# Where a kernel makes its last weight parts: eight in place of six behind the first batch's units

## The chip, the cores and the metric

The kernel runs on one core of a Trainium2 chip. The metric is the device time of one execution in microseconds (us). The engines are named as in the profile: PE is TensorE (PEld its weight loads), DVE is VectorE, ACT is ScalarE, POOL is GpSimd, SP is SyncE, which here only issues DMAs. Each engine works through its own list of instructions in the order written down at build time, and waits where an instruction's inputs or buffers aren't ready.

## What is computed

The input x has 8 batches of 3008 tokens with 256 channels. A real Fourier transform runs along the tokens, a complex 256 x 256 product with a bias and a soft threshold acts on the spectrum, and the inverse transform gives the tokens back. A feed-forward layer follows, with the square of a ReLU between its two products.

```python
X = np.fft.rfft(x, axis=1)
Yr = Xr @ w_r - Xi @ w_i + b_r
Yi = Xr @ w_i + Xi @ w_r + b_i
Yr = np.sign(Yr) * np.maximum(np.abs(Yr) - 0.01, 0.0)
Yi = np.sign(Yi) * np.maximum(np.abs(Yi) - 0.01, 0.0)
y = np.fft.irfft(Yr + 1j * Yi, n=3008, axis=1)
h = y.reshape(24064, 256) @ w_in          # 256 x 2048
out = np.maximum(h, 0.0) ** 2 @ w_out     # 2048 x 256
```

The weights w_in and w_out come as 64-bit floats.

## The kernel before

**The transforms.** 3008 is 64 x 47, so each transform is two stages of small matrix products with a pass through device memory between them. Batch 0 comes first and alone: seven `Fwd32` loads (`ring`) make its first stage, and 24 units (`Unit32`) do the rest, each with a load (`ka`), a forward product (`fwd`, L401), copies (`bins`), the mix with the weights (L415), the threshold on DVE (`shrink`, tiles `kv` and `kc`), and the way back (`back`, L426) with a store of two halves (`kuh`, `kul`) into the array `s3`. Later batches do the same as `Fwd` or `Fwd2` tasks and as pairs of units (`Pair`), spread as jobs with due times in half steps between the feed-forward work of the batch before. For batch 1, `Fwd2` runs thirteen times (L352): the first five directly behind the units, from x loaded early (`x6`), the other eight in the first tile, from the two buffers of `xt`.

**The feed-forward layer.** Each batch is cut into six tiles of some 500 tokens. `Back` loads a tile's data from s3 (`du`), makes the last stage of the inverse transform on PE (L461, L464, L465), and ACT and DVE write it to `yr` (through `dy`). `Tokens` forms the sums (`ms`) and the two halves (`yt`) that the products need; for the first tile DVE does this, for the others POOL. A tile has eight steps and each step two half steps, `first` and `second`: seven products in the manner of Strassen-Winograd, each of three matmuls, out of `win` into the banks `psh`. DVE reads these (`mp`, `mu`, `mv`, `mc`), ACT makes ReLU, square and a rounded copy (`mg`), POOL the rest of `mg`. `out` of step n, two steps later, multiplies with `wout` into `pso`. The steps' own instructions are chained in order on each engine by `then`.

**The weights.** w_in and w_out are cut into 16 parts of 128 x 512, in the order of the list `parts`: two of w_in, two of w_out, and so on. A part (`Double`) is loaded as 64-bit values (512 KB, tile `dst`, tag `big`, four buffers), and `convert(n, after)` makes 32-bit floats of it. `bits` is one ACT and four DVE instructions (L148 to L155), `join` two on DVE (L159 and L163), after which the loaded tile is no longer needed. A part of w_out is then split into a rounded half and a rest (`split`, one instruction on ACT and one on DVE). For w_in this is done for two parts at a time (`win_sums`): four sums (`ds`) and three splits, seven instructions on DVE and three on ACT. `after` names a unit or step: `bits` is then placed behind that step's last DVE and ACT instruction (`cut` and `done`).

**Which part is made when.** Parts 0 and 1 are made before the units. `EARLY` and `LATE` set the rest: with `LATE = 6`, parts 2 to 9 are made behind every second unit (`paced`, turns 3 to 17 of the loop at L670), parts 10 to 12 behind the last unit, and parts 13, 14 and 15 behind half steps 1, 3 and 5 of the first tile (`LATER`). Parts 10 to 13 are loaded in turns 20 to 23 of the units' loop, each placed behind the load of a unit or of the last one; parts 14 and 15 are loaded behind the first tile's loads of `du`. All loads in question are on SP's queue, and those made through `load_next` (L106) are kept in one order: each is placed behind the one before it in `chain`. The loads of `xt`, and the `du` loads of later tiles, come behind the last weight loads in that chain.

**Memory and order.** A tag has a fixed number of buffers (`FRONT`, `MAIN`), and a tile takes a buffer when the last reader of the tile before is done. The weights' scratch lies in a pool `conv`; when the last part is placed the pool is closed (L748), and its memory goes to the tiles of the pairs and of `Fwd` named in `SIDE`. A planner turns the program into one list for each engine: of the instructions that are ready by its own estimate of time, it takes the one that stands first in the program, and obeys `issue_after`.

Of the kernel before, what the change touches and what calls it, by code (L numbers as in the profile page):

```python
# [58 lines left out]
def fnet_moe(ctx: ExitStack, tc, x, w_r, w_i, b_r, b_i, w_in, w_out, bm, cm, dx, a32, c32, out):  # L59
# [21 lines left out]
    def memory(stack, name, **kwargs):  # L81
        return stack.enter_context(tc.tile_pool(name=name, bufs=2, reuse_waits="tile", **kwargs))
# [89 lines left out]
    def moe_part(q):  # L172
        if q < 8:
            f, c = divmod(q, 2)
            return Double(
                None, None, w_in[c * 128:(c + 1) * 128, f * 1024:(f + 1) * 1024],
                lambda t: t.rearrange("p f t -> p (f t)"),
            )
        f = (q - 8) * 2
        return Double(  # L180
            wout[0][:, f:f + 2], wout[1][:, f:f + 2],
            w_out[f * 128:(f + 2) * 128, :].rearrange("(f p) d -> p f d", p=128),
            lambda t: t.rearrange("p (f d) t -> p f (d t)", f=2),
        )


    def win_sums(n, parts):
        (a11, a21), (a12, a22) = (
            [w[:, :, f] for f in range(2)]
            for w in (p.w.rearrange("p (n f d) -> p n f d", n=2, f=2) for p in parts)  # L190
        )
        st = T("ds", [128, 2, 4, 128], F32)
        s1, s2, s3, s4 = (st[:, :, j] for j in range(4))
        dve.tensor_add(out=s1, in0=a21, in1=a22)
        sub(dve, s2, s1, a11)
        sub(dve, s3, a11, a21)
        sub(dve, s4, a12, s2)
        hi, lo = (w[:, 2 * n:2 * n + 2] for w in win)
        halves(hi[:, :, A11], lo[:, :, A11], a11, dve)
        halves(hi[:, :, A12:A22 + 1], lo[:, :, A12:A22 + 1], parts[1].w.rearrange("p (n f d) -> p n f d", n=2, f=2), dve)  # L200
        halves(hi[:, :, S1:], lo[:, :, S1:], st, dve)
# [386 lines left out]
    def pair_tasks(pairs, start, step, end=7.1):  # L588
        jobs = []
        for j, u in enumerate(pairs):  # L590
            at = start + j * step
            if j:
                jobs += [(at - 3.7, u.load)]
            jobs += [
                (at, u.fwd), (at + 1.0, u.sums), (at + 3.7, u.load_back),
                (at + 2.1, lambda u=u: u.mix(1)), (at + 3.0, lambda u=u: u.mix(0)), (at + 4.0, u.shrink),
                (at + end, lambda u=u: u.back(0)), (at + end + 0.9, lambda u=u: u.back(1)),
            ]
        return jobs

    def fwd_tasks(b, start, step):
        jobs = []
        for q in range(J):
            f, at = Fwd(b, q), start + q * step
            jobs += [(at - 2.5, f.load), (at - 0.8, f.add), (at + 0.3, f.run)]
        return jobs

    def back_tasks(t, start):
        b, c0, h = tiles[t]
        new = range(-(-c0 // W2), -(-(c0 + 2 * h) // W2))  # L610
        jobs = []
        for j, q in enumerate(new):
            k, at = Back(b, q), start + 2.2 * j
            jobs += [(at, k.load), (at + 1.6, k.mm)]
            if len(k.spans) > 1:
                jobs += [(start + 14.6, k.put)]
        k = Tokens(t)
        for j in range(2):
            jobs += [(start + 7.1 + j, lambda j=j: k.sums(j))]
        for j in range(4):  # L620
            jobs += [(start + 9.1 + 1.2 * j, lambda j=j: k.split(j))]
        return jobs
# [8 lines left out]
    parts = [moe_part(q) for q in (0, 1, 8, 9, 2, 3, 10, 11, 4, 5, 12, 13, 6, 7, 14, 15)]  # L631
# [9 lines left out]
        b32 = load_mix_weights()  # L641


    EARLY, LATE = 2, 6
    LATER = {1: 13, 3: 14, 5: 15}

    def convert(n, after=None):
        p = parts[n]
        p.bits(after)
        p.join()  # L650
        if n % 4 > 1:
            p.split()
        elif n % 4:
            win_sums(n // 4, parts[n - 1:n + 1])
# [6 lines left out]
    for n in range(EARLY):  # L661
        convert(n)
    paced = [(n, 2 * (n - EARLY)) for n in range(EARLY, len(parts) - LATE)]
    loads = [(k - 1, parts[n]) for n, k in paced] + [(20 + j, p) for j, p in enumerate(parts[-LATE:-2])]

    PRE = 5
    nam = T("nam", [M1, M1], F32)
# [2 lines left out]
    for r in range(-5, len(units) + 3):  # L670
# [10 lines left out]
        while loads and loads[0][0] <= r:  # L681
            p = loads.pop(0)[1]
# [16 lines left out]
    steps = [Step(t, n) for t in range(len(tiles)) for n in range(NF // 2)]  # L699
    slots = len(HALF) * NF  # L700
    first = sorted(back_tasks(0, 0), key=lambda j: j[0])
    for name in ("load", "mm", None):
        for _, job in first:
            if (job.__name__ if job.__name__ in ("load", "mm") else None) == name:
                job()
        for p in parts[-2:] if name == "load" else ():
            with tc.issue_after(chain[nc.sync].ins):
                p.load()
            chain[nc.sync] = p.get
    for n in range(len(parts) - LATE, min(LATER.values())):  # L710
        convert(n, units[-1])
    nam = T("nam", [M1, M1], F32)
    act.mul(nam, am32[:, 1], -1.0)
# [3 lines left out]
    for m in range(2 * len(steps) + 4):  # L717
        b, r = divmod(m, slots)
        if r == 0 and b < B:
            jobs = [(t - slots, job) for t, job in jobs]  # L720
            if b + 1 < B:
                first, step, end = 1.0, 6.1, 7.1
                if b == 0:
                    first, step, end = 11.2, 5.3, 9.1
                    for q in range(PRE, J):
                        if q > PRE + 1:
                            jobs += [(0.9 * (q - PRE - 2), second[q].load)]
                        jobs += [(0.5 + 0.9 * (q - PRE), second[q].run)]
                    jobs += [(first - 0.6, pairs[1][0].load)]
                jobs += pair_tasks(pairs[b + 1], first, step, end)  # L730
            if b + 2 < B:
                first, step = (2.6, 7.0) if b else (14.6, 6.0)
                jobs += fwd_tasks(b + 2, first, step) + [(95.0, pairs[b + 2][0].load)]
            for j in range(len(HALF)):
                t = b * len(HALF) + j + 1
                if t < len(tiles):
                    jobs += back_tasks(t, NF * j + 0.5)
            jobs.sort(key=lambda j: j[0])
        n, k = divmod(m, 2)
        if k and 0 <= n - 2 < len(steps):  # L740
            steps[n - 2].out(1)
        if n < len(steps):
            (steps[n].second if k else steps[n].first)()
        if not k and 0 <= n - 2 < len(steps):
            steps[n - 2].out(0)
        if m in LATER:
            convert(LATER[m], steps[n])
        if m == max(LATER):  # L748
            conv.close()
            pools.update(dict.fromkeys(CONV), **dict.fromkeys(SIDE, memory(ctx, "side")))  # L750
        while jobs and jobs[0][0] < r + 1:
            jobs.pop(0)[1]()
# [86 lines left out]
```

## Time and profile before

| | us |
|---|---|
| median of 3 runs | 2615.43 |
| lowest and highest | 2613.71, 2618.53 |
| the profiled execution | 2614.82 |
| its span in the profile | 2613.1 |

The profiled execution is the one from which all rows come. A row of the timeline gives start, duration, engine (PEq, SPq and so on are the queues that issue), line, operation, what is written from what, the shapes, how many instructions the row holds, and in brackets how long the engine had been idle before it and what released it. A line can be that of a helper: L97, L98 and L101 are the copies and the subtraction that every part of the kernel calls, and L484 is `then`. A row of the view by stages gives busy time in a stretch. Each matmul of 32-bit floats outside the steps shows as two matmuls in a row.

### The profile page before, as it was taken

The page shows a single profiled execution, that of the slowest core. Times are in us where ns is not written, and L with a number is a line of the kernel's source. Part 1 is how long each engine was busy: PE and PEld are TensorE (multiplying, and loading weights), DVE is VectorE, ACT ScalarE, POOL GpSimd, SP SyncE. Part 2 cuts the span into 40 slices and gives each one's busy share as a digit, 9 for nine tenths or more (in the row PEclk, how much of TensorE's full clock was granted, in tenths as well). Part 3 has the DMA queues.
Part 4 walks back from the last instruction along what each step waited for, and adds up shares of the span by engine and source line. Part 5 has one row for each costly group of instructions (what it writes and reads, how often), then busy time and mean ns, then how long its engine had stood idle before and what let it go on. Part 6 is the DMA issues. An engine that isn't in the chain of part 4 may idle for free.

```text
span 2613.1 us, 47540 instructions
## 1 busy us (share of the span) xinstructions
PE 2564.3 (98%) x16908; PEld 2347.0 (90%) x16908; DVE 1782.3 (68%) x3797; ACT 1672.7 (64%) x2434; POOL 1657.0 (63%) x1628
## 2 busy tenths in 40 slices
PE   6799999999999999999999999999999999999999
PEld 4689989999999999999999999999999999999998
DVE  6877766667767767577676776667676677765554
ACT  3556656666666666666666666666666666666665
POOL 2246666766766667667666676666667666666564
PEclk8999999999999999999999999999999999999999
DMA  8733332333332332233332333323332223221100
GB/s 267 236 110 110 102 113 82 95 106 107 95 91 75 116 104 86 84 95 113 104 92 82 97 110 100 99 76 101 103 108 80 71 79 101 71 65 41 33 17 17
DMA packets 191455, 250.51 MB, mean 96 GB/s; under 512 B 21755, under 2 KB 135923, under 8 KB 191219
## 3 DMA queue, kind: packets, MB, share of 16 engines
q1 hardware_dynamic: 178240, 223.89, 28.1%
q0 software_dynamic: 12304, 22.35, 3.6%
q8 instruction: 136, 2.23, 0.4%
q10 hardware_dynamic: 675, 1.23, 0.2%
q14 instruction: 100, 0.82, 0.1%
HBM read 146.85 MB, written 100.53 MB: 95 GB/s over the span
## 4 chain that ended last, share of the span: by engine, by line
PE 84%; POOL 1%; DMA 1%; issue 0%; DVE 0%; ACT 0%; POOLq 0%; SPq 0%; ACTq 0%; DVEq 0%
PE pso L484 36%; PE psh L484 32%; PE psf L301 6%; PE psf L280 2%; PE psf L236 2%; PE psf L333 2%; PE psf L464 1%; PE psf L465 1%; PE psf L461 1%; DMA du<-s 1%; POOL mg L101 0%; POOL yt L101 0%; POOL ms L101 0%; POOL ms L500 0%; ACT mc L484 0%
## 5 line engine op out<-in xcount | busy, mean ns | idle before, releaser
L101 POOL TENSOR_TENSOR mg<-mc,mg 128x500 fp32r<-128x500 f32 (+1 forms) x768 | 975.0, 1290 | 594.3 <-ACT mg L97 549.7
L484 PE MATMUL pso<-mg,wout 128*128 128x500 f32 (+1 forms) x4608 | 1176.2, 392 | 1.8 <-ACT mg L97 1.3
L484 PE MATMUL psh<-yt,win 128*128 128x250 f32 (+1 forms) x8064 | 1072.9, 281 | 1.5 <-DVE mc L484 1.2
L484 ACT ACTIVATE mc<-mc 128x1000 f32<-128x1000 f32 (+1 forms) x768 | 802.6, 1045 | 406.6 <-DVE mc L484 397.3
L484 PEld LDWEIGHTS psh<-yt,win 128*128 128x128 f32 x8064 | 1022.2, 189 | 34.3 <-PE psh L484 1.9
L484 PEld LDWEIGHTS pso<-mg,wout 128*128 128x128 f32 x4608 | 818.7, 189 | 130.0 <-POOL mg L101 1.9
L484 DVE TENSOR_TENSOR mc<-psh,mv 128x500 f32<-128x500 f32 (+3 forms) x768 | 419.1, 547 | 428.1 <-PE psh L484 395.4
L97 ACT CAST mg<-mc 128x1000 fp32r<-128x1000 f32 (+1 forms) x384 | 396.9, 1034 | 18.4 <-ACT mc L484 0.4
L484 DVE TENSOR_TENSOR mv<-psh,mu 128x500 f32<-128x500 f32 (+1 forms) x384 | 260.6, 679 | 53.5 <-PE psh L484 21.8
L301 PE MATMUL psf<-wx,kxh 128*128 128x256 f32 x1008 | 206.7, 281 | 2.4 <-ACT kxh L97 1.7
L98 DVE COPY mp<-psh 128x250 f32<-128x250 f32 (+1 forms) x384 | 159.7, 416 | 39.2 <-PE psh L484 16.2
L301 PEld LDWEIGHTS psf<-wx,kxh 128*128 128x128 f32 x1008 | 166.3, 189 | 6.7 <-ACT kxh L97 1.9
L101 POOL TENSOR_TENSOR ksl<-kv,ksh 128x512 fp32r<-128x512 f32 x84 | 108.8, 1295 | 94.6 <-ACT ksh L97 94.5
L484 DVE TENSOR_TENSOR mu<-psh,mp 128x250 f32<-128x250 f32 (+1 forms) x384 | 160.5, 418 | 11.5
L215 POOL TENSOR_TENSOR xs<-xt 120x256 f32<-120x256 f32 x156 | 115.4, 760 | 72.5 <-DMA xt<-x_in 67.6
L484 DVE TENSOR_TENSOR mc<-psh,mp 128x250 f32<-128x250 f32 (+1 forms) x384 | 156.8, 408 | 4.3 <-PE psh L484 2.8
L322 DVE TENSOR_TENSOR kv<-psf,ke 64x256 f32<-64x256 f32 x336 | 141.8, 422 | 22.9 <-PE psf L301 14.2
L301 PE MATMUL psf<-wx,kxl 128*128 128x256 f32 x504 | 141.1, 280 | 1.0 <-DVE kxl L101 1.0
L97 ACT COPY dy<-psf 128x188 f32<-128x188 f32 x256 | 76.9, 313 | 82.7 <-PE psf L465 82.2
L313 DVE TENSOR_TENSOR ke<-psf,bias 128x512 f32<-128x512 f32 x84 | 58.0, 691 | 102.0 <-PE psf L301 101.9
L97 ACT CAST ksh<-kv 128x512 fp32r<-128x512 f32 x84 | 52.0, 619 | 114.3 <-DVE kv L101 113.4
L97 ACT CAST kuh<-psf 128x256 fp32r<-128x256 f32 x192 | 68.4, 372 | 88.2 <-PE psf L333 71.4
(102 smaller groups left out, 2565.4 us busy)
## 6 DMA issues: line engine op xcount, KB each, us to landing
du<-s SPq DMA_DIRECT2D x128, 256.0 KB, 2.9
s<-kuh SPq DMA_DIRECT2D x192, 128.0 KB, 1.8
s<-kul SPq DMA_DIRECT2D x192, 128.0 KB, 1.8
kcm<-cm_in POOLq DMA_DIRECT2D x84, 256.0 KB, 3.3
ka<-s SPq DMA_DIRECT2D x84, 256.0 KB, 3.4
s<-xe SPq DMA_DIRECT2D x87, 240.0 KB, 2.4
xt<-x_in SPq DMA_DIRECT2D x86, 240.0 KB, 3.3
du<-s SPq DMA_DIRECT2D x256, 64.0 KB, 2.8
```

What stands on the lines that cost most here:

```text
L97: return act.copy(out=out, in_=in_)
L98: return eng.tensor_copy(out=out, in_=in_)
L101: return eng.tensor_tensor(out=out, in0=a, in1=b, op=ALU.subtract)
L215: return eng.tensor_tensor(out=out[:, :n], in0=self.xt[:, :n, 0], in1=self.xt[:, :n, 1], op=(ALU.add, ALU.subtract)[t])
L236: nc.tensor.matmul(ps[:M1, t], am32[:, t], self.u[:, t], start=True, stop=True)
L280: nc.tensor.matmul(pv[:, :, c, g, :], self.a[:, g, c * 128:(c + 1) * 128], bg, start=True, stop=True)
L301: self.last = nc.tensor.matmul(ps, l, wx[j][:, k, c, :], start=n == 0, stop=n == 5)
L313: dve.tensor_add(out=self.e, in0=self.pe, in1=bias)
L322: dve.tensor_add(out=v[64 * r:64 * r + 64, g], in0=ps[gs], in1=self.e[gs, r])
L333: nc.tensor.matmul(ps[:, :D], self.cm[:, g, j * 128:(j + 1) * 128], r[:, g], start=n == 0, stop=n == 2)
L461: mm = nc.tensor.matmul(pv[:, :, 0], self.u[:, 0, cs], dx_sb[:, 0], start=True, stop=False)
L484: last_of[eng] = op(*args, **kwargs)
```

## The change

Parts 8 and 9, a pair of w_in, are no longer made between the units. `LATE` becomes 8, and `LATER` holds lists of parts. Parts 8 to 10 are made behind the last unit, part 11 behind half step 1 of the first tile, the pair 12 and 13 behind half step 3, part 14 behind half step 5 and part 15 behind half step 7. Parts 8 to 11 are loaded in turns 18 to 21 of the units' loop, and the last four parts behind the first tile's `du` loads. The pool `conv` is closed behind half step 7.

```diff
-    EARLY, LATE = 2, 6
-    LATER = {1: 13, 3: 14, 5: 15}
+    EARLY, LATE = 2, 8
+    LATER = {1: (11,), 3: (12, 13), 5: (14,), 7: (15,)}
...
-    loads = [(k - 1, parts[n]) for n, k in paced] + [(20 + j, p) for j, p in enumerate(parts[-LATE:-2])]
+    loads = [(k - 1, parts[n]) for n, k in paced] + [(18 + j, p) for j, p in enumerate(parts[-LATE:-LATE + 4])]
...
-        for p in parts[-2:] if name == "load" else ():
+        for p in parts[4 - LATE:] if name == "load" else ():
             with tc.issue_after(chain[nc.sync].ins):
                 p.load()
             chain[nc.sync] = p.get
-    for n in range(len(parts) - LATE, min(LATER.values())):
+    for n in range(len(parts) - LATE, min(LATER.values())[0]):
         convert(n, units[-1])
...
-        if m in LATER:
-            convert(LATER[m], steps[n])
+        for p in LATER.get(m, ()):
+            convert(p, steps[n])
         if m == max(LATER):
             conv.close()
```

## The prediction

> **What bounds the kernel now.** First the page's first part, for which engine sets the time.
>
> ```profile
> span 2613.1 us, 47540 instructions
> PE 2564.3 (98%) x16908; PEld 2347.0 (90%) x16908; DVE 1782.3 (68%) x3797; ACT 1672.7 (64%) x2434; POOL 1657.0 (63%) x1628
> ```
>
> TensorE (PE) is busy 2564.3 of 2613.1 us. The change adds and removes no matmul, so only the 48.8 us in which PE is idle, or runs at a reduced clock, can move. The view of busy time by stages tells where they are (columns: stretch, its length, then PE, PEld, DVE, ACT, POOL busy, granted clock, DMA share, GB/s).
>
> ```profile
> 60.00:82.00 22.00, 18.05 (x91) 15.73 (x92) 21.98 (x48) 11.91 (x34) 6.41 (x6) 1.00 0.91 283
> 82.00:110.50 28.50, 25.91 (x131) 22.34 (x130) 23.39 (x54) 13.78 (x41) 10.76 (x10) 1.00 0.71 227
> 110.50:119.40 8.90, 8.90 (x44) 7.56 (x43) 8.62 (x19) 5.66 (x11) 0.00 (x0) 1.00 0.70 217
> 119.40:130.60 11.20, 3.83 (x21) 3.09 (x19) 8.35 (x22) 4.92 (x13) 0.28 (x1) 0.74 0.75 227
> 130.60:136.10 5.50, 5.47 (x16) 4.32 (x17) 0.00 (x1) 0.59 (x1) 0.00 (x0) 0.60 0.11 26
> 136.10:187.50 51.40, 50.85 (x321) 45.77 (x320) 42.18 (x83) 33.79 (x48) 28.66 (x27) 1.00 0.45 131
> 355.00:366.00 11.00, 6.50 (x37) 5.52 (x36) 5.21 (x11) 6.11 (x11) 10.98 (x13) 0.89 0.58 162
> 366.00:2613.10 2247.10, 2239.70 (x14985) 2061.68 (x14984) 1512.62 (x3235) 1466.62 (x2065) 1475.99 (x1446) 1.00 0.29 86
> ```
>
> Up to 110.5 the units of batch 0 run; VectorE (DVE) is full from 60 to 82, but over 82 to 110.5 PE is short of only 2.6 us. From 110.5 to 130.6 lies the passage to the first tile. From 136.1 on PE is all but full: 0.55 us idle in the first tile's 51.4 us, 7.4 us in the last 2247. So the change can win at most what PE loses between 82 and 136, and it can lose in the first tile.
>
> **What leaves the units.** Parts 8 and 9 go from between the units to behind them. In the trace they run on DVE from 82.05 to 99.1, between the units' own work (tile kv); the second row below is that work alone. The three rows are the DVE rows of the view by stages: all, then the instructions on kv, then all in the passage.
>
> ```profile
> 82.05:99.10 17.05, 16.57 (x38) 1.00 0.77 237
> ...
> 82.05:99.10 17.05, 7.66 (x18) 1.00 0.77 237
> ...
> 110.45:121.35 10.90, 10.52 (x22) 1.00 0.71 213
> ```
>
> Of the 38 instructions, 18 are on kv and one is the last of part 7; the other 19 (six for each part, seven for the sums of the pair) take 16.57 - 7.66 - 0.7 = 8.2 us. DVE gives up 8.2 us here. PE does not gain as much, since it is already near its own pace:
>
> ```profile
> 86.75 0.67 PE L426 MATMUL psf<-kv,kk 128*128 128x256 f32 x2 [0.43 <-DVE kv L101]
> ...
> 92.67 0.67 PE L426 MATMUL psf<-kv,kk 128*128 128x256 f32 x2 [0.33 <-issue]
> ...
> 97.95 0.60 PE L426 MATMUL psf<-kv,kk 128*128 128x256 f32 x2
> ...
> 100.56 0.60 PE L426 MATMUL psf<-kv,kk 128*128 128x256 f32 x2
> ...
> 104.08 0.70 PE L426 MATMUL psf<-kv,kk 128*128 128x256 f32 x2 [0.75 <-ACT ku L97]
> ...
> 110.06 0.67 PE L426 MATMUL psf<-kv,kk 128*128 128x256 f32 x2 [0.96 <-DVE kv L101]
> 110.56 1.46 PE L352 MATMUL psf<-x,am 120*120 120x256 f32 x6
> 111.86 0.59 PE L352 MATMUL psf<-x,nam 120*120 120x256 f32 x2
> 112.29 1.46 PE L352 MATMUL psf<-x,am 120*120 120x256 f32 x6
> ```
>
> From 97.95 to 100.56 a unit costs 2.6 us with PE never waiting. The last gap (0.96) is the latency of the last unit's shrink and stays. The others shown, with some smaller ones, make 2.6 - 0.96 = 1.6 us. The 0.75 us at 104 waits for ScalarE, itself behind stores; loads of four parts still go out together behind the last unit's load, so that gap may stay. I take **-1.2 us** for this stage (between 0 and -2.6). Two 512 KB loads also leave this stage; I give them nothing of their own, since the gaps above already hold what they could win.
>
> **The passage.** Between the last unit and the first tile DVE did parts 10, 11 and 12 (the 22 instructions of the last row above, two of them kul: 20 in 10.1 us, 0.5 us each) and then two instructions of part 13. It now gets parts 8 and 9 with the seven sums, and 10: 26 instructions against 22, +2.0 us. It is not laid on the path whole. Behind the L352 runs, the path goes through the first tile's inverse transform:
>
> ```profile
> 122.61 0.36 PE L461 MATMUL psf<-dx_sb,du 128*128 128x188 f32 x1 [2.60 <-DVE yr L471]
> ...
> 124.39 0.33 PE L461 MATMUL psf<-dx_sb,du 128*128 128x188 f32 x1 [0.83 <-DMA du<-s]
> ```
>
> At 122.61 PE waited for DVE, which had been on weights until then; at 124.39 it waited 0.83 us for a transfer all the same. So 0.8 us more on DVE would be hidden there, and DVE itself waits again afterwards. In this stage DVE is busy 8.35 of 11.2 us, so 2.85 us are free, and 2.0 are added, low in priority against the tile's own work. I take **+0.8 us**: half an instruction of delay at a few places. Bounds: -1.7 (if the weights no longer stand ahead of yr at 122) and +2.0 (all on the path).
>
> **The first tile.** Parts 11 to 15 replace 13 to 15 here. The whole DVE, and then its step work fed from psh, in the stretch where 13 to 15 are made:
>
> ```profile
> 143.40:169.00 25.60, 24.99 (x45) 1.00 0.40 112
> ...
> 143.40:169.00 25.60, 8.02 (x18) 1.00 0.40 112
> ```
>
> 45 - 18 - 2 (yr, 0.5 us) = 25 weight instructions in 16.5 us: 0.66 us each, against 0.5 in the passage. Added are seven for part 11, six for 12 and the two of 13 that had slipped into the passage: 15, so 7.5 us (at 0.5) to 9.9 us (at 0.66). DVE has 51.4 - 42.2 = 9.2 us free from 136.1 to 187.5, and all 5.5 us from 130.6 to 136.1. This last hole exists because PE did two L352 runs of batch 1 (16 matmuls) before it went on with step 0; they waited for x, loaded at 125.00:
>
> ```profile
> 123.88 1.03 SPq L139 DMA_DIRECT2D dst<-w_out_in  x2
> 125.00 9.72 SPq L108 DMA_DIRECT2D xt<-x_in  x3
> ...
> 143.57 0.33 SPq L108 DMA_DIRECT2D xt<-x_in  x1
> ...
> 160.83 1.48 SPq L108 DMA_DIRECT2D du<-s  x3
> ...
> 176.31 0.42 DVE L98 COPY mp<-psh 128x252 f32<-128x252 f32 x1
> ...
> 169.63 1.11 POOL L108 DMA_DIRECT2D kcm<-cm_in  x2
> ...
> 177.86 0.39 SPq L108 DMA_DIRECT2D ka<-s  x1
> ```
>
> That order cannot stay. Four loads of weights now stand where two stood, and there are four buffers for them (tag big). Parts 8 to 11 fill these, so the load of part 15 has to wait until part 11 is joined, which is put behind step 0. The loads of x are chained behind it on SP, so the L352 runs must come after step 0, and steps 0 and 1 start some 5 us sooner. DVE so has 9.2 + 5.5 = 14.7 us for the 7.5 to 9.9 us added: it fits. PE's total work is the same, and what was two L352 runs at a clock of 0.60 (5.5 us for what takes 3.5 at 110.56) becomes step work at that clock, an even trade. Parts 12 and 13 together keep DVE from steps 2 and 3 for a time, while fewer L352 runs are at hand to fill PE; for that I take **+2 us** (between -2, if the earlier steps pay, and the slower cases below). All weights are in time: 12 and 13 are wanted by step 6, whose step work on DVE comes at 176.31 us, and 14 and 15 by outputs later still. The memory of the weights goes over to the pairs of batch 1 (names in SIDE) two half steps later: kcm at 169.63 on POOL's queue may be held until part 15 is done, ka at 177.86 on SP's by little; the pairs' first matmul comes after both, and I cost this at nothing as long as part 15 is done by 178, else at what it is late.
>
> **Sum.** -1.2 + 0.8 + 2.0 = +1.6 us. The profiled execution took 2614.8 us (1.7 around its span), so 2616.4; it lies 0.6 below the median of the three runs, so against that median **2617.0 us**. 0.2% is 5.2 us, about what a measurement can tell from no change.
>
> **A rule that speaks against the change.** In the first tile GpSimd (POOL) runs beside the weights, which the units' stage has less of. Mean times of one instruction in the first tile and then in the passage, where POOL did nothing:
>
> ```profile
> L151 DVE TENSOR_SCALAR da<-da 128x512 f32<-128x512 f32 x3 | 3.1, 1023 | 0.3 <-ACT da L148 0.3
> ...
> L151 DVE TENSOR_SCALAR da<-da 128x512 f32<-128x512 f32 x3 | 1.3, 425 | 0.3
> ```
>
> The instruction takes 2.4 times as long in the first tile, so a part moved there costs more than it did. The Trainium skill, page "SBUF — State Buffer", section "Who interferes with whom", says that VectorE's two-port modes and its instructions with two SBUF inputs share a port pair with GpSimd, and that the one that starts second blocks fully until the first ends; these two rows agree. By that rule alone, with every added instruction meeting POOL, rival C is what comes out.
>
> **Rivals.**
> A, *the units were DVE-bound after all*, and the passage loses its wait: then -2.6 and -1.7 and a gain of 2 in the first tile, 2615.4 - 6.3 = **2609**. For it: DVE full at 60 to 82. Against: PE's own 2.6 us a unit.
> B, *SP's queue*, on the slower side: the load of part 15 holds back x and, in the same chain, the tile-1 loads of du. A join took 8.4 us from the end of its step in the trace:
>
> ```profile
> 139.48 0.41 DVE L484 TENSOR_TENSOR mc<-psh,mp 128x252 f32<-128x252 f32 x1
> ...
> 147.63 0.68 DVE L159 SCALAR_TENSOR_TENSOR dw<-dst,da 128x512 f32<-128x512 uint32 x1
> ...
> 179.70 1.28 POOL L101 TENSOR_TENSOR yt<-ms,yt 128x504 fp32r<-128x504 f32 x1 [0.28 <-ACT yt L97]
> ...
> 185.55 1.81 PE L484 MATMUL psh<-yt,win 128*128 128x252 f32 x14
> ```
>
> With step 0 done near 135, x is loaded near 143.5 in place of 125.0: 18.5 us late. Tile 1's yt was ready at 181.0, and PE wants it at 186.6 (nine of the 14 matmuls at 185.55 still belong to tile 0): 5.6 us of slack. If nothing is caught up, PE stands 18.5 - 5.6 = 12.9 us; two buffers of x allow two runs in about 7 us, by which six runs before the last du load need 21 and put it at 164, 3 us late and hidden. It decides when the delay of that load passes 5.6 us. I price it at half, 6.5 us: 2615.4 - 0.4 + 6.5 = **2621.5**.
> C, *DVE runs out in the first tile*: if all 15 added instructions are slowed as L151 is, they take 15 x 0.5 x 2.4 = 18.0 us where 14.7 are free, and PE waits the other 3.3 us on top of the forecast: **2620.3**. For it: the 24.99 of 25.60 us above. Against: the mean of 0.66 us that holds for the 25 weight instructions there.
>
> **How the numbers follow.** Forecast 0.57 (2611 to 2620.5), A 0.14, B 0.16, C 0.13. The idle 4.5 us at 355 to 366 hang on the order that the planner writes down and may go or double: that widens both ends. Range 2609 to 2625: A's and B's times with the 12.9 us end of B cut short. Faster by over 0.2% (below 2610.2): A, 0.14. Slower by over 0.2% (above 2620.7): B and about half of C with a little of the forecast's own tail, 0.25. Within: 0.61.
>
> **What would show it.** Units: the last L426 at 108.5 to 109.5, not 110.06. Passage: yr near 121 to 122. First tile: no L352 ahead of step 0's end, DVE at work from 131 to 136, the load of part 15 followed by x near 143; PE idle of 2 to 3 us between 131 and 160. B shows as PE waiting for yt or a DMA near 185; C as PE waiting for DVE (mv, mc) between 145 and 160. I am wrong at the root if the last L426 comes before 107, or if time moved behind 366.

## The result, and the profile after

| | before | after |
|---|---|---|
| median, us | 2616.98 (4 runs) | 2638.09 (4 runs) |
| lowest and highest, us | 2613.71, 2618.68 | 2631.76, 2638.41 |
| profiled execution, us | 2614.82 | 2638.41 |

The changed kernel is slower: the ratio of the times is 1.0074, with a 95% interval of 1.0062 to 1.0086, or 21.1 us by the medians. The forecast was 2617.0 us and the range ended at 2625.0; the time lies 13 us above it.

The first part of the page of the changed kernel:

```profile
span 2636.6 us, 47544 instructions
PE 2571.0 (98%) x16908; PEld 2351.1 (89%) x16908; DVE 1789.4 (68%) x3797; ACT 1674.2 (63%) x2434; POOL 1658.7 (63%) x1628
```

The span grew by 23.5 us, PE's busy time by 6.7 us with the same matmuls, so PE ran longer at a reduced clock (granted 0.97 and 0.96 in the two stages from 136.1 to 355, 1.00 in both before). The other 16.8 us are idle time of PE (65.6 against 48.8). The stages say where (the view by stages of the changed kernel, columns as in the prediction), and the last row is the one stretch of the kernel before that the prediction left out:

```profile
60.00:82.00 22.00, 17.68 (x89) 15.41 (x90) 21.99 (x48) 11.94 (x35) 6.45 (x6) 1.00 0.74 228
82.00:110.50 28.50, 26.57 (x137) 23.31 (x137) 15.56 (x38) 11.75 (x40) 7.27 (x10) 1.00 0.75 235
119.40:130.60 11.20, 4.64 (x23) 3.73 (x22) 9.12 (x22) 5.62 (x13) 0.29 (x1) 0.70 0.67 215
130.60:136.10 5.50, 5.50 (x33) 5.50 (x34) 3.91 (x9) 1.27 (x2) 0.00 (x0) 0.67 0.01 3
136.10:187.50 51.40, 45.11 (x256) 38.96 (x255) 44.23 (x81) 29.11 (x40) 20.57 (x15) 0.97 0.38 111
187.50:355.00 167.50, 157.44 (x1031) 143.88 (x1030) 109.40 (x228) 99.28 (x149) 103.53 (x105) 0.96 0.35 101
366.00:2613.10 2247.10, 2239.23 (x14991) 2061.85 (x14990) 1522.13 (x3246) 1469.30 (x2075) 1485.39 (x1458) 1.00 0.29 87
```

```profile
187.50:355.00 167.50, 166.67 (x1132) 154.04 (x1131) 119.74 (x253) 106.90 (x159) 106.42 (x108) 1.00 0.34 101
```

Up to 136 nothing is lost. Then PE is idle 6.3 us in the first tile (0.55 before) and 10.1 us up to 355 (0.8 before), and it makes 65 matmuls less in the one and 101 less in the other. Behind 366 the two kernels run alike.

The timeline of SP's issues in the changed kernel shows the cause at one glance:

```profile
122.93 0.98 SPq L139 DMA_DIRECT2D dst<-w_in_in  x2
124.02 20.08 SPq L139 DMA_DIRECT2D dst<-w_out_in  x2
144.19 8.16 SPq L108 DMA_DIRECT2D xt<-x_in  x3
...
154.51 0.54 SPq L108 DMA_DIRECT2D xt<-x_in  x1
...
167.80 0.33 SPq L108 DMA_DIRECT2D xt<-x_in  x1
...
183.06 1.48 SPq L108 DMA_DIRECT2D du<-s  x3
...
197.71 0.39 SPq L108 DMA_DIRECT2D ka<-s  x1
```

The two loads of parts 14 and 15 make one row of 20.08 us: the first goes out at once, the second waits on the queue. It waits for part 11, whose loaded tile DVE reads for the last time here (DVE's timeline):

```profile
142.49 1.17 DVE L159 SCALAR_TENSOR_TENSOR dw<-dst,da 128x512 f32<-128x512 uint32 x1
```

The read ends at 143.66, and x goes out, 19.2 us later than before (144.19 against 125.00). The last du load of tile 1 is 22.2 us late (183.06 against 160.83) and ka, the first load of batch 1's pairs, 19.9 us (197.71 against 177.86). What stood behind the waiting load was held back, and none of it was caught up.

The rows of PE's timeline that follow a wait, with the row that makes the first x run:

```profile
129.81 8.66 PE L484 MATMUL psh<-yt,win 128*128 128x252 f32 x51 [2.59 <-ACT yt L97]
...
145.53 0.94 PE L484 MATMUL psh<-yt,win 128*128 128x252 f32 x6 [2.24 <-DVE mc L484]
...
150.10 1.46 PE L352 MATMUL psf<-xt,am 120*120 120x256 f32 x6
...
164.45 2.47 PE L352 MATMUL psf<-xt,am 120*120 120x256 f32 x6 [3.52 <-DVE yr L471]
...
198.94 0.79 PE L484 MATMUL psh<-yt,win 128*128 128x252 f32 x2 [5.65 <-ACT yt L97]
200.97 2.05 PE L280 MATMUL psf<-kb,ka 128*128 128x128 f32 x8 [1.24 <-DMA kb<-bm_in]
```

At 145.5 the runs of L352 that used to fill the gaps between steps aren't there, at 164.5 PE waits for DVE, which is on weights, and at 198.9 for yt of tile 1, which is made from the late du. The clock is reduced behind the long gap: the view by stages has it at 0.50 from 200 to 206, and the eight L280 matmuls, which take 2.05 us here, took half of that in the trace of before:

```profile
194.44 1.05 PE L280 MATMUL psf<-kb,ka 128*128 128x128 f32 x8
```

### The profile page after: what moved, and what is told of

It reads as the page before. It is cut to its first block, busy times and chain, and to the rows that moved or that the text cites. A ratio compares the mean times of both kernels' runs of the same rounds, so it can differ in the third digit from the quotient of the medians.

```text
span 2636.6 us, 47544 instructions
## 1 busy us (share of the span) xinstructions
PE 2571.0 (98%) x16908; PEld 2351.1 (89%) x16908; DVE 1789.4 (68%) x3797; ACT 1674.2 (63%) x2434; POOL 1658.7 (63%) x1628
## 4 chain that ended last, share of the span: by engine, by line
PE 92%; DVE 3%; DMA 2%; ACT 1%; issue 1%; POOL 1%; SPq 0%; POOLq 0%; ACTq 0%; DVEq 0%
PE pso L484 39%; PE psh L484 34%; PE psf L301 7%; PE psf L280 3%; PE psf L236 2%; PE psf L333 2%; PE psf L464 1%; PE psf L465 1%; PE psf L461 1%; PE psf L415 1%; DMA s<-xe 1%; DMA x<-x_in 0%; PE psf L352 0%; DVE df L152 0%; ACT mc L484 0%
## 5 line engine op out<-in xcount | busy, mean ns | idle before, releaser
L484 DVE TENSOR_TENSOR mv<-psh,mu 128x500 f32<-128x500 f32 (+1 forms) x384 | 260.7, 679 | 53.1 <-PE psh L484 21.8
L322 DVE TENSOR_TENSOR kv<-psf,ke 64x256 f32<-64x256 f32 x336 | 141.8, 422 | 17.5 <-PE psf L301 10.2
```

The lines of the kernel that those rows point to most:

```text
L322: dve.tensor_add(out=v[64 * r:64 * r + 64, g], in0=ps[gs], in1=self.e[gs, r])
L484: last_of[eng] = op(*args, **kwargs)
```

## The experiments

Two theories stood after the result. **Q (the queue)**: the load of part 15 waits on SP and holds back all that is behind it. **D (DVE)**: five parts in the first tile are too many for DVE. The profiled runs are compared by the time at which a step begins (the start of its first DVE instruction, the copy of `mp` from `psh`). Here is how many us later than in the profiled run of the kernel before each kernel came to it, taken from the timelines (a minus is earlier; steps 0 to 7 are the first tile, 8 and 24 begin tiles 1 and 3):

| step | after | e1 | e2 | e3 | e4 | e5 | e6 | e7 | e8 | e9 | e10 |
|---|---|---|---|---|---|---|---|---|---|---|---|
| 0 | -5.7 | -7.7 | -2.8 | -7.3 | 3.8 | -5.1 | -7.3 | -4.3 | 0.4 | -2.1 | -4.9 |
| 3 | -10.4 | -3.5 | -4.1 | -12.4 | 3.2 | -2.1 | -3.3 | -4.1 | -0.1 | -1.1 | -10.2 |
| 8 | 17.3 | 7.6 | 5.8 | 13.2 | 3.2 | 7.4 | -1.3 | -4.1 | -0.1 | -1.1 | 10.1 |
| 24 | 21.4 | 5.5 | 6.3 | 14.2 | 3.1 | 9.1 | -1.3 | -4.1 | 0.2 | -1.1 | 17.6 |
| 48 | 24.0 | 4.1 | 6.9 | 14.7 | 11.1 | 10.5 | 5.9 | -3.0 | 3.1 | 1.9 | 19.3 |

In the changed kernel the loss is made between steps 3 and 24; at step 3 it is even ahead, since work of L352 has been put off. e3, which has the wait and no part more, goes the same way. A column is one execution: the profiled ones of e1 and e3 lie 5.4 us under the medians of their runs, that of e4 3.8 us over it. So a few us in a column, in the lower rows above all, may be chance. Times in the next table are medians; the ratios are against runs of the kernel before on the same chip.

| | median, us | ratio | before, us |
|---|---|---|---|
| e1_own_buffer | 2623.10 (10 runs) | 1.0024 [1.0014, 1.0033] | 2616.43 (21 runs) |
| e2_late_load | 2626.13 (6) | 1.0033 [1.0022, 1.0045] | the same |
| e3_before_blocked | 2633.96 (4) | 1.0062 [1.0047, 1.0078] | the same |
| e4_five_in_passage | 2621.37 (10) | 1.0021 [1.0011, 1.0030] | the same |
| e5_one_per_step | 2625.45 (6) | 1.0032 [1.0020, 1.0043] | 2617.02 (28) |
| e6_no_dve_14_15 | 2621.46 (11) | 1.0017 [1.0008, 1.0026] | the same |
| e7_x_first | 2612.95 (11) | 0.9982 [0.9973, 0.9991] | the same |
| e8_own_control | 2616.28 (11) | 0.9999 [0.9990, 1.0008] | the same |
| e9_four_late | 2617.51 (11) | 1.0004 [0.9995, 1.0013] | 2617.08 (15) |
| e10_changed_x_first | 2632.09 (5) | 1.0059 [1.0046, 1.0071] | the same |

### The wait taken away: e1 and e2

e1 is the changed kernel with a buffer of its own for part 15:

```diff
+    "own": 1,                 # in FRONT, and "own" in CONV
-            self.st = T("dst", [128, 512, 2], I32, tag="big")
+            self.st = T("dst", [128, 512, 2], I32, tag=getattr(self, "tag", "big"))
+    parts[15].tag = "own"
```

> The changed kernel, with a buffer of its own for the load of part 15, so that this load waits for nothing and holds nothing back on SP's queue; the weights are made in the same places. Queue theory (the load of part 15 waits on SP's queue for part 11 and holds back x and du, and that is most of the 21 us): 2614 to 2622 us, x for L352 issued near 126 and not 144, tile 1 started within 4 us of the kernel before. DVE theory (15 more weight instructions in the first tile starve PE): 2632 us or more, with PE waiting for DVE between 140 and 175. If both share it, it lies between, and the distance to 2616 is DVE's share.

e2 leaves the buffers and puts the load of part 15 later in the chain, at half step 5, behind the loads of x that are due by then:

```diff
-        for p in parts[4 - LATE:] if name == "load" else ():
+        for p in parts[4 - LATE:-1] if name == "load" else ():
...
+        if m == 5:
+            with tc.issue_after(chain[nc.sync].ins):
+                parts[-1].load()
+            chain[nc.sync] = parts[-1].get
         for p in LATER.get(m, ()):
```

> The changed kernel, with the load of part 15 placed behind the loads that are due up to half step 5, so that most loads of x and of tile 1's du go first; buffers and the places of the weights as in the changed kernel. Queue theory: 2614 to 2622 us, as with a buffer of its own. DVE theory: 2632 us or more. A third theory, that any new order written by the planner costs such amounts by chance, would have the two remedies far apart from each other.

Against the changed kernel's 2638.09 us, e1 is 15.0 us and e2 12.0 us faster. Both lie above Q's range (2614 to 2622), e2 by 4 us, and far below D's. They are 3.0 us apart, which speaks against the third theory of e2's text, that any new order costs such amounts by chance. On SP's timeline the block is gone in both; e1 first, then e2:

```profile
121.49 0.89 SPq L139 DMA_DIRECT2D dst<-w_out_in  x2
122.48 12.50 SPq L108 DMA_DIRECT2D xt<-x_in  x3
...
160.54 1.48 SPq L108 DMA_DIRECT2D du<-s  x3
```

```profile
123.37 10.80 SPq L108 DMA_DIRECT2D xt<-x_in  x3
...
165.97 1.48 SPq L108 DMA_DIRECT2D du<-s  x3
167.50 0.59 SPq L139 DMA_DIRECT2D dst<-w_out_in  x1
```

In e1 the last du goes out at 160.54, as it did before, and yet 6.7 us remain lost. So the queue is most of the loss but not all of it.

### The wait alone: e3 and e8

e3 is the kernel before, its parts and their places unchanged, in which parts 13 and 15 share one buffer. The load of part 15 so waits on SP for the join of part 13. e8 is its control: the extra buffer, but for part 15 alone, so that nothing waits. Both have the other lines of e1's edit too.

```diff
+    parts[13].tag = parts[15].tag = "own"   # e3
+    parts[15].tag = "own"                   # e8
```

> The kernel before (six late parts), in which parts 13 and 15 share one buffer of their own: the load of part 15 then waits on SP's queue until part 13, behind half step 1, is joined, as in the changed kernel it waits for part 11. No weight work is moved. Queue theory: 2628 to 2640 us, x for L352 near 144, tile 1 late by 10 us or more. DVE theory: 2613 to 2619 us.

> The kernel before with a buffer of its own for the load of part 15 and no other change: a control for the blocked run, since one buffer more moves the memory and lets the planner write another order. Queue theory: 2614 to 2619 us, so that the blocked run's 2634.0 stands as the price of the wait. If it comes out over 2625, the blocked run proves nothing.

e8 is the kernel before to 0.1% (0.9999), so the buffer costs nothing. e3 is 17.7 us slower than e8, which ran on another chip, and 17.5 slower than the kernel before on its own, with a 95% interval of some 12 to 20 us by the ratio. No instruction is added on any engine. Its SP timeline, and below it PE's:

```profile
121.99 20.50 SPq L139 DMA_DIRECT2D dst<-w_out_in  x2
142.60 8.12 SPq L108 DMA_DIRECT2D xt<-x_in  x3
...
182.35 1.48 SPq L108 DMA_DIRECT2D du<-s  x3
```

```profile
143.89 0.94 PE L484 MATMUL psh<-yt,win 128*128 128x252 f32 x6 [2.24 <-DVE mc L484]
...
160.12 0.94 PE L484 MATMUL psh<-yt,win 128*128 128x252 f32 x6 [1.36 <-DVE mc L484]
...
198.11 2.05 PE L280 MATMUL psf<-kb,ka 128*128 128x128 f32 x8 [6.57 <-DMA kb<-bm_in]
```

One row of 20.50 us on SP makes the same picture as in the changed kernel. The two waits for mc are to be noted: they are named for DVE, and the 2.24 us of the changed kernel at 145.5 is there to the digit, but e3 has no part more than the kernel before in this tile. PE waits for DVE here because it has no run of L352 to do in the meantime. A wait named for an engine isn't yet a proof that this engine has too much to do.

Queue and DVE all but add up: 17.7 us (e3 against e8) and 6.7 us (e1) are 24.4, against 21.1 measured; by the profiled runs at step 24, 14.2 and 5.5 are 19.7, against 21.4. Both agree within the interval of e3 alone.

### What is left without the wait: e4, e5 and e6

e4 makes all of parts 8 to 12 behind the last unit, and in the first tile only 13, 14 and 15, as the kernel before does.

```diff
+    LATER = {1: (13,), 3: (14,), 5: (15,)}     # LATE = 8, loads as changed
```

> Eight late parts, but 8 to 12 all behind the last unit and only 13, 14, 15 in the first tile, as in the kernel before. The load of part 15 then waits for part 11 no longer than the passage. It prices the passage alone: 17 to 19 weight instructions more there than before at 0.43 us are 7 to 8 us, less 2 to 3 us of idle DVE and 1 us won in the units: both theories 2616 to 2623 us; over 2628 would say that neither is the whole.

It loses 3.2 us by step 3, no more up to step 24, and more again behind that; by the medians it is 4.9 us slower than before. PE's row shows that the passage does hide little, the wait for yr growing from 2.60 us to 6.08:

```profile
126.67 0.52 PE L461 MATMUL psf<-dx_sb,du 128*128 128x188 f32 x1 [6.08 <-DVE yr L471]
```

e5 is e1 with the parts spread, one every second half step, so that 12 and 13 no longer stand in a row.

```diff
+    LATER = {1: (11,), 3: (12,), 5: (13,), 7: (14,), 9: (15,)}
```

> The changed kernel with the own buffer for part 15, and the weights of the first tile one part behind each of the half steps 1, 3, 5, 7, 9, in place of 12 and 13 together. If the 7 us left over the kernel before (2623.1 against 2616.4) come from DVE being kept from the steps by 12 and 13 in a row: 2618 to 2621 us and less PE idle between 135 and 195 than the 6.2 us of the own-buffer run. If they don't: 2622 to 2626.

Spreading didn't help: 8.4 us above the kernel before, against e1's 6.7. So the rest of the loss doesn't hang on the pair standing in a row. It goes with the number of parts: from step 3 to step 24 of the table the kernels with three parts in the first tile and no wait on SP (e4, e7, e8, e9) lose 0.3 us at most, those with five 9.0 (e1), 10.4 (e2) and 11.2 us (e5).

e6 is e1 in which parts 14 and 15 are not made: for each, two ScalarE copies of the upper words stand in for the conversion, and seven DVE instructions are left out.

```diff
         p = parts[n]
+        if n > 13:
+            with tc.issue_after(after.done.ins):
+                for w in (p.hi, p.lo):
+                    copy(act, w, p.st[:, :, 1].bitcast(F32).rearrange("p (f d) -> p f d", f=2))
+            return
```

> The changed kernel with the own buffer, in which parts 14 and 15 are not made: ScalarE copies the upper words of the loaded values to both halves, two instructions for two, and their 14 DVE instructions are left out, so that the first tile holds about as much weight work on DVE (26 instructions) as the kernel before (25). If DVE's load is what is left: 2615 to 2619 us. If it is the planner's other order or the passage: 2621 to 2625.

The table by steps is clear here: e1 and e6 come to step 3 alike (3.5 and 3.3 us ahead, with the same matmuls done), and at step 24 e6, without these 14 instructions, is 1.3 us ahead of the kernel before, e1 5.5 us behind. So DVE's added work costs 6.8 us up to there. The medians don't show it: e6 is 4.4 us above the kernel before where e1 is 6.7, the two intervals overlap, and 2621.46 lies in the range that was set for the planner's other order or the passage. In e6's profiled run the gain is gone again by step 48. The view by stages of e6 shows one place: from 355 to 366 PE is busy only 4.48 us (6.50 before), and in the timeline PE waits there for ScalarE.

```profile
136.10:187.50 51.40, 49.56 (x313) 44.72 (x312) 39.32 (x79) 34.86 (x52) 29.46 (x28) 1.00 0.46 132
...
355.00:366.00 11.00, 4.48 (x21) 3.72 (x22) 8.74 (x10) 4.34 (x8) 8.37 (x10) 0.64 0.46 132
```

Why a kernel that comes to this stretch earlier waits longer in it wasn't tried. e8's profiled run, too, loses 2 to 3 us there, with a median like before's, so the stretch moves by that much without any change of the parts.

Where did the free time go that DVE had by the prediction? e1 shows it, in DVE's timeline:

```profile
136.98 1.03 DVE L151 TENSOR_SCALAR da<-da 128x512 f32<-128x512 f32 x1 [3.83 <-ACT da L148]
...
148.01 1.03 DVE L151 TENSOR_SCALAR da<-da 128x512 f32<-128x512 f32 x1 [0.90 <-ACT da L148]
```

DVE stands idle for 3.83 us ahead of the first instruction of part 11 that needs ScalarE, because ScalarE's instruction is placed behind step 0's last (`done`). Behind 148 DVE has no gap left, and PE waits for its mc, 1.82 and 0.91 us. In PE's timeline of e1:

```profile
161.89 0.96 PE L484 MATMUL psh<-yt,win 128*128 128x252 f32 x6 [1.82 <-DVE mc L484]
...
177.55 0.94 PE L484 MATMUL psh<-yt,win 128*128 128x252 f32 x6 [0.91 <-DVE mc L484]
...
186.40 1.13 PE L280 MATMUL psf<-kb,ka 128*128 128x128 f32 x8 [1.80 <-DMA kb<-bm_in]
```

### The lesson used: e7, e9 and e10

If loads behind a weight load are what hurts, the kernel before may suffer from it too: its x waits behind two loads of weights. e7 is the kernel before with the loads of parts 14 and 15 behind the first two loads of x.

```diff
-        for p in parts[-2:] if name == "load" else ():
-            with tc.issue_after(chain[nc.sync].ins):
-                p.load()
-            chain[nc.sync] = p.get
...
         second[q].load()
+    for p in parts[-2:]:
+        with tc.issue_after(chain[nc.sync].ins):
+            p.load()
+        chain[nc.sync] = p.get
```

> The kernel before, with the loads of parts 14 and 15 behind the first two loads of xt on SP's queue and not ahead of them. The x for the two L352 runs then need not share the engines with 1 MB of weights: they should land near 127 and not 130.6, and PE, idle from 127.4 to 130.6, can run them there. 2612.5 to 2615 us if that wait counts, 2616 to 2617 if the first tile's yt is as late as x anyway.

This beats both kernels: 2612.95 us, a ratio of 0.9982 [0.9973, 0.9991]. SP's timeline and then PE's:

```profile
123.19 0.98 SPq L108 DMA_DIRECT2D xt<-x_in  x2
124.29 0.91 SPq L139 DMA_DIRECT2D dst<-w_out_in  x2
...
156.76 1.48 SPq L108 DMA_DIRECT2D du<-s  x3
```

```profile
126.46 2.77 PE L352 MATMUL psf<-xt,am 120*120 120x256 f32 x6
...
131.84 2.44 PE L484 MATMUL psh<-yt,win 128*128 128x252 f32 x18
```

The first run of x starts at 126.46 without a wait. In PE's timeline of before this row was:

```profile
130.63 2.89 PE L352 MATMUL psf<-xt,am 120*120 120x256 f32 x6 [3.27 <-DVE yt L101]
```

The brackets name DVE's yt, which was done at the same time, but L352 doesn't read yt. It reads x, which landed 5.5 us after its issue there (the median of three loads, issued from 125.00 on) and 3.1 us after it in e7. Step 0 follows at 131.84 in place of 136.11, and the 4.1 us are kept up to tile 3.

e9 is e7 with `LATE = 4`, so that two parts more are made between the units.

```diff
-    EARLY, LATE = 2, 6
+    EARLY, LATE = 2, 4
     LATER = {1: 13, 3: 14, 5: 15}
```

> The change turned the other way, on top of x first: four late parts in place of six. Parts 10 and 11 are made between the units (turns 19 and 21), 12 behind the last unit, 13 to 15 in the first tile as in the kernel before. If PE sets the pace of the units from 82 us on and DVE has room there, the passage loses 14 weight instructions (about 7 us of DVE) and yr no longer waits behind them: 1 to 2.6 us below x first (2613.0), so 2610 to 2612. If the units' stage is bound by DVE after all: 2615 to 2620.

It gives all of e7's gain back (2617.51 us), which is the range that was set for units bound by DVE. Its view by stages tells why for the larger part; DVE has next to no gap left between the units:

```profile
82.00:110.50 28.50, 24.54 (x119) 20.82 (x120) 28.08 (x61) 14.75 (x42) 7.72 (x9) 1.00 0.66 212
```

From the back product (L426) of the eleventh unit to that of the twentieth PE takes 29.81 us here and 27.05 in e7. At step 24 e9 is some 3 us behind e7; the other 2 us come in the stretch about 355 again, and are open.

e10 is the changed kernel with the same edit as e7, for its last four parts. The first two loads of x are then free; the others, and du, still stand behind the load that waits.

```diff
-        for p in parts[4 - LATE:] if name == "load" else ():
...
         second[q].load()
+    for p in parts[4 - LATE:]:
+        with tc.issue_after(chain[nc.sync].ins):
+            p.load()
+        chain[nc.sync] = p.get
```

> The changed kernel, with the loads of parts 12 to 15 behind the first two loads of xt. The load of part 15 still waits for part 11, now ahead of the other six loads of x and of tile 1's du only. If it is these later loads that cost (tile 1's yt comes late): 2628 to 2638 us, though the first two L352 runs come near 127. If the delay of the first two x is what costs: 2614 to 2624.

2632.09 us, so only 6 of the 21 us are won. The SP rows show the wait in its new place:

```profile
122.19 0.98 SPq L108 DMA_DIRECT2D xt<-x_in  x2
...
145.66 0.40 SPq L139 DMA_DIRECT2D dst<-w_out_in  x1
146.15 0.41 SPq L108 DMA_DIRECT2D xt<-x_in  x1
...
174.76 1.89 SPq L108 DMA_DIRECT2D du<-s  x3
```

## Why the prediction was wrong

**The units, right.** The last L426 was forecast at 108.5 to 109.5. In the trace of after:

```profile
109.01 0.67 PE L426 MATMUL psf<-kv,kk 128*128 128x256 f32 x2 [0.96 <-DVE kv L101]
```

That is 1.05 us sooner, against the 1.2 taken. DVE's row of the view by stages, for the stretch in which parts 8 and 9 had been:

```profile
82.05:99.10 17.05, 8.92 (x23) 1.00 0.85 253
```

DVE was relieved by 7.65 us (16.57 before), and PE gained 1.05. By itself that gain is not clear of chance: e3 and e7, with parts 8 and 9 where the kernel before has them, reach this row 1.73 and 0.95 us sooner too. The pace is clearer: from the eleventh unit's L426 to the twentieth's PE takes 27.06 us in the trace of before, 27.05 in e7 and e8 and 27.65 in e3, but 25.43 in the changed kernel and in e1. So the stage gains about 1.6 us there, a fifth of what DVE was relieved by, and rival A falls: with parts 8 and 9 gone, PE set this stage, not DVE. e9 shows the other side, where two parts more do make DVE the bound.

**The passage, right.** From the last L426 to step 0's matmuls PE took 20.8 us (109.01 to 129.81) against 20.6 up to the point where it went on before (130.63); +0.8 was taken, +0.2 came. e4 shows that this was near the end of what can be hidden: with two parts more in the passage, the wait for yr grows by 3.5 us, and 3.2 of them are lost at step 3.

**The order on SP, right up to x.** No L352 came before step 0, and x went out at 144.19, with 143.5 forecast. (In e1 step 0 comes first too, though x waits for nothing there, so the wait alone doesn't make that order.)

**What became of the late x: the step that failed.** Rival B held the mechanism, and priced it at 12.9 us "if nothing is caught up", which is 2627.9 us and beyond the stated range. The forecast's own sum has no term for it, because the prediction let it catch up: "two buffers of x allow two runs in about 7 us, by which six runs before the last du load need 21 and put it at 164, 3 us late and hidden". It went out at 183.06. From the first load of x to this load it took 38.9 us, against 35.8 in the trace of before (125.00 to 160.83). It took 38.1 in e1 and 33.6 in e7, 39.8 in e3 and 42.6 in e2: with x early or late, this stretch is never near 21 us. The runs of L352 are written into PE's list between the steps, and each buffer of x is free only behind such a run, so the steps set the pace and not the two buffers. The trace of before could have told it: 35.8 us for these loads stand in the prediction's own rows. With them, x at 143.5 puts the du load at 179.3, 18.5 us late and not 3, and B at its full 12.9. The du load was 22.2 us late in fact; less 5.6 of slack that is 16.6, and B comes to some 2632 us. e3 measures the mechanism by itself at 17.7.

The prediction also asked only when yt would be ready. A second consumer hangs on the same loads: ka is read from what the last run of L352 stores (L225), and was 19.9 us late. In e3 it is for kb, issued right behind ka, that PE waits longest (6.57 us, to 198.11); tile 1's yt is done there at 197.94, so the two come late together. And the sum took PE's own time as fixed ("PE's total work is the same"): behind such waits it grew by 6.7 us at the lower clock.

**The first tile, right in sign and too small.** +2.0 us was taken, bounded upward by C. Without the wait on SP, e1 goes from 3.5 us ahead at step 3 to 5.5 behind at step 24, a loss of 9.0 us, and e6 puts 6.8 us on the 14 instructions of two parts. The price of an instruction was about right; the view of costliest groups in the first tile (137 to 176) of after has L150 to L163 at 0.73 us on the mean (21.8 us for 30 instructions in six rows; the same rows in the trace of before have 12.8 us for 18, 0.71). Two of the six:

```profile
L159 DVE SCALAR_TENSOR_TENSOR dw<-dst,da 128x512 f32<-128x512 uint32 x5 | 5.3, 1081 | 0.0
...
L151 DVE TENSOR_SCALAR da<-da 128x512 f32<-128x512 f32 x5 | 3.7, 748 | 0.3 <-ACT da L148 0.3
```

L151 was slowed less than in the trace of before (1023 ns), L159 more (683 ns there). The Trainium skill, page "SBUF — State Buffer", section "Who interferes with whom", has an instruction of VectorE that reads two SBUF inputs (as L159 does) or runs in a two-port mode use a port pair that it shares with GpSimd, and whichever of the two starts second waits for the other. A delay that moves so from one instruction to another agrees with that, though no run here shows it by itself. Rival C as worded, with every instruction slowed 2.4 times, did not happen; what went wrong was the other side of the sum, "14.7 us" free on DVE. That was idle time of a stage added up, and in e1 4.7 us of it were spent waiting for ScalarE's first instruction of a part, ahead of the steps in which DVE was then short.

**The memory that goes over to the pairs, right.** It was costed at nothing if part 15 is done by 178. Its last instruction ran at 174.09 for 0.68 us, and ka was late because of the stores of L225, not because of the memory.

**What stays open.** Why the stretch about 355 to 366 (steps 24 to 32), and in e4 and e6 steps 40 to 48, cost between nothing and 4.5 us in one kernel and not in another, and so why the medians of e1 and e6 show only 2.2 us of the 6.8. How the 6.7 us that e1 keeps by its median divide between DVE's work in the first tile and the planner's other order is therefore shown by single traces up to step 24, and not by the times.

## What to carry to other kernels

Before a load is added to an in-order queue, ask which buffer it waits for and what stands behind it: a load that waits for a buffer belongs behind the loads that the next stage needs, or gets a buffer of its own. A late transfer is not caught up by having two buffers if the work that frees them is written between other work at a fixed pace; read that pace from the trace, from the first to the last load of the series. Idle time of an engine summed over a stage isn't room: look at where in its list the holes are, and what ends them.

## What the runs showed of the hardware

A load on SP that waits for a buffer is not marked as a wait in the timeline. Where it is merged with its neighbour, the one row covers the wait (20.08 and 20.50 us); where it stands by itself, as in e10, it shows its own 0.40 us, and the wait is the hole before it. The queue behind it stands still for all of that time, although the loads behind it have free buffers (x went out at 144.19 in the changed kernel, and its first two loads at 122.19 in e10). And in these traces a gap of PE cost more than its length: around the 6.57 us gap of e3 and the 5.65 us gap of the changed kernel the granted clock was 0.50 (195 to 200 and 198 to 206), eight L280 matmuls took 2.05 us in place of 1.05, and of the 23.5 us lost 6.7 are PE's longer busy time.
